# A fused attention, experts and MLP kernel: attention's score products on four 64x64 array tiles, its two heads in two PSUM banks, and a reordered word list

## The chip, the cores and the metric

The kernel runs on one core of a Trainium2 chip. Its time is the device time of one execution in microseconds (us); lower is better. The core has a matrix engine (PE), a vector engine (DVE), a scalar engine (ACT), a third elementwise engine (POOL), and queues of DMA transfers, most of them issued by SP. PE writes its results into PSUM, which has eight banks (0 to 7) of 128 partitions by 512 float32; the other engines read them from there.

## What is computed

Three stages run one after the other in one program, all float32.

```python
# 1. attention: 2 batches, 8 heads, 768 positions, head size 64
k_sum = k.reshape(B, H, 24, 32, D).max(axis=3)          # block maxima of the keys
v_sum = v.reshape(B, H, 24, 32, D).mean(axis=3)         # block means of the values
scores = scale * concat(q @ k.T where |i-j| < 16, q @ k_sum.T) (+ log 32 on the blocks)
x = softmax(scores) @ concat(v, v_sum)                  # 1536 tokens x 512
# 2. four experts, all used: x 512 -> 1024 -> 512, p = domain_probs / their sum
x = sum over e of p[:, e] * (max(x @ w1[e], 0) @ w2[e])
# 3. MLP 512 -> 2048 -> 512
h = x @ w_in;  out = (h * sigmoid(1.702 * h)) @ w_out
```

## The kernel before

**Attention in groups.** Four windows of 64 queries of one pair of heads are a *group*; there are 24 (g = 0 to 23, half of them of the first batch). The two heads of a pair lie on the partition halves 0 to 63 and 64 to 127 of queries and keys. A window of 64 queries needs 96 keys around it and 24 block maxima, so a window's scores have 120 columns. One group goes through these steps, each of them a *word* of the program:

- `sc g` (line 253, PE): eight score products, 4 windows by 2 heads, each 64x64 by 64x120. For groups 0 to 3 two words do this in parts, `dl` with the 96 window columns and `dm` with the 24 block columns (line 270).
- `msk g` (DVE, line 282): reads the scores from PSUM, scales them and adds the mask; then the row maximum (line 287).
- `exp g` (ACT, line 294), `ad g` and `rec g` (the inverse of the sum), `mul g` (DVE or POOL as the letter behind it says, line 314).
- `T g` (PE, line 322): four transposes; `aT g` (ACT, line 328) copies them out.
- `V g` (PE, line 338): eight value products of 64 columns; `xh g` (ACT, line 352) copies them out; `low g` (DVE, line 359) makes the low part for the first batch.
- The block means of the values come by `mp` (POOL), `mq` (DVE), `mt` (PE, line 230), `mk` (ACT), and `vb g` (POOL, line 238) spreads them into the operand of `V g`.

**The experts between them.** While attention of the second batch is still under way, the first expert runs on the first batch: `f i.k` (and `e`, line 455) are first products of hidden unit i, three matmuls each; `ga i` (DVE, line 406), `hh i` (ACT, line 472) and `hl i` (POOL or DVE, line 412) make the gated hidden values and split them into a high and a low part; `s i.d` (line 494) are second products: high by high weights, then low by high weights, then high by low weights. So an `s` needs `hl` from its second matmul on. K, Q, U, N, M, Y, WA and WC are loads on the SP queue; `q0` to `q6` are the first products of the next expert. `x1` words are products whose result nobody reads.

**What sets the order.** A string `ORDER` of 761 words is run from front to back, and each word emits its instructions. Each engine carries out its own instructions in the order in which they were emitted; across engines they wait by semaphores. The framework puts the waits in: who writes a tile in PSUM waits for those who still read the tile's earlier contents.

**Banks.** Scores of all groups but 1 and 2 are in bank 5, head 0 on its upper and head 1 on its lower partition half, so the products use the two array tiles on the diagonal: rows 0 to 63 with columns 0 to 63, rows 64 to 127 with columns 64 to 127. Transposes are in bank 6, value products and the second batch's means in bank 7, the first batch's means and the hidden units from the fifth on (`hidden_bank`) in bank 4. The main part after attention has its two product banks X and Y in 6 and 7.

Of the kernel before, what the change touches and what calls it, by code (L numbers as in the profile page):

```python
# [8 lines left out]
F32 = mybir.dt.float32  # L9
# [4 lines left out]
ALU = mybir.AluOpType  # L14
# [31 lines left out]
def attention_moe_mlp(ctx, tc, kq, vw, vT, dpT, wts, w64, out):  # L46
# [13 lines left out]

    def bank(n, name):
        return psum.tile([P, 512], F32, tag=f"bank{n}", name=name)
# [21 lines left out]
    NM = GW + 2  # L84
# [13 lines left out]
    nc.gpsimd.memset(mask[:, 0, 0 : RAD - 1], NEG)  # L98
    nc.gpsimd.memset(mask[:, NM - 1, WIN + RAD - 1 : KW], NEG)

# [126 lines left out]
    xo = {}  # L227

# [30 lines left out]

    def direct_products(g, c0, c1):  # L260
        b, hp, w0 = g
        k, q = kts[b, hp], qs[g]
        if c0 == 0:
            scs[g] = bank({1: 3, 2: 2}.get(groups.index(g), 5), f"sc{b}{hp}{w0}")
        ps = scs[g]
        for j in range(GW):
            w = (w0 + j) * WIN
            for h in range(2):
                r = slice(h * D, (h + 1) * D)
                nc.tensor.matmul(  # L270
                    ps[r, j * KA + c0 : j * KA + c1],
                    q[r, j * WIN : (j + 1) * WIN],
                    kss[b, hp][r] if c0 else k[r, w : w + KW],
                    start=True, stop=True,
                )

    def masked(g):
# [4 lines left out]
        nc.vector.scalar_tensor_tensor(  # L282
            out=s, in0=ps[:, 0 : GW * KA].rearrange("p (j c) -> p j c", c=KA),
            scalar=1.0 / math.sqrt(D), in1=mask[:, m0 : m0 + GW, :], op0=ALU.mult, op1=ALU.add,
        )
# [45 lines left out]
    def value_products(g):  # L331
        b, hp, w0 = g
        a = st.pop(g)
        v = vs.pop(g)
        ps = st[g] = xo["ps"] = bank(7, f"xo{b}{hp}{w0}")
        for j in range(GW):
            for h in range(2):
                nc.tensor.matmul(  # L338
                    ps[h * D : (h + 1) * D, j * WIN : (j + 1) * WIN],
                    v[0:KA, j, h * D : (h + 1) * D],  # L340
                    a[0:KA, j * P + h * WIN : j * P + (h + 1) * WIN],
                    start=True, stop=True,
                )
# [97 lines left out]
    def hidden_bank(i):  # L441
        return i if i < EARLY else 4
# [318 lines left out]
    def pair(j, extras):  # L761
# [49 lines left out]
        x, y = bank(6, f"X{j}"), bank(7, f"Y{j}")  # L811
# [23 lines left out]
        x = bank(6, f"X{j}b")  # L835
# [22 lines left out]
    def outputs(j, tiles):  # L858
# [62 lines left out]
        def of_half(h):  # L921
# [5 lines left out]
            if h == 0:  # L927
                o = bank(7, "rest")[:, 0 : DM // 2]
# [51 lines left out]
    wlA5:v V5 vb6 ad7:s T6 mk3 gm xh5 vb7 low5 f4.1 aT6 vb8 ps rec7 e2.2 mul7:v win8 e2.3 wb8 win9  # L980
    e2.1 wb9 Q9 pb V6 T7 xh6 sc8 low6 aT7 whC1:s V7 msk8 whC0:s wlC1:g e2.0 xh7 f4.2 low7 exp8
# [17 lines left out]
    T18 sc20 xh16 V17 aT18 hl9:g hl10:g msk20 exp19 Q22 f11.0 ad19:g s8.1 s8.2 f11.1 exp20 win21
    rec19 s8.3 mul19:v U21 f11.2 vb18 win22 f11.3 s9.0 ga11 s9.1 ad20:s s9.2 f12.0 wb21 hh11 hl11:v  # L1000
    ph1 rec20 ph3 xh17 wb22 s9.3 T19 mul20:g sc21 pl3:v aT19 T20 V18 msk21 ph2 xh18 sc22 V19 aT20
    pl1:v Q23 exp21 pc Sa2 win23 wb23 U22 f12.1 vb20 s10.0 U23 msk22 f12.2 f12.3 wBh1 xh19 exp22
    ga12 ad21:g rec21 mul21:v ph0 hh12 sc23 V20 T21 xh20 msk23 f13.0 f13.1 vb21 f13.2 aT21 f13.3
    wBl1:v ad22:g s10.1 rec22 mul22:v exp23 s10.2 ga13 Sa0 ad23:s V21 hh13 pl2:g T22 vb22 rec23
    f14.0 s10.3 mul23:g xh21 f14.1 f14.2 aT22 f14.3 T23 V22 s11.0 aT23 vb23 xh22 hl13:v hl12:v ga14
    V23 pl0:g s11.1 hh14 s11.2 s11.3 xh23 hl14:v f15.0 wo2:v s12.0 s12.1 wo0:v s12.2 wo1:v s12.3
    wo3:v f15.1 f15.2 ra2 s13.0 s13.1 d0 kp d1 f15.3 q0 s13.2 th0 s13.3 s14.0 d2 th1 ga15 q1 tl0:v
    s14.1 mv0 s14.2 hh15 th2 s14.3 tl1:v hl15:g tt0 Ph0 q2 tl2:v d3 mv1 s15.0 s15.1 eu0 eu1 q3 th4
    Sa1 tg0 mv2 Sa3 tl4:v q4 s15.2 tt1 q5 Ph2 wBh0 tg2 eu2 Ph3 Pl2 tr2 tg1 tr0 wBl0:v q6 tw2:v tt2
    Pl0 tr1 Ph1 tw1:g s15.3 tg3 tr3 rb1 Pl3:v eu3 Pl1:v tw3:g tw0:g  # L1010
    """

    xh[0] = slot("xh0", [P, KC, S], F32R, "xh0")
# [287 lines left out]
```

## Time and profile before

| | |
|---|---|
| time, median of 3 runs | 825.35 us (825.27 to 825.8) |
| span of the profiled execution (first to last instruction) | 824.2 us |
| what lies around the span, against the median | 1.15 us |
| PE busy | 817.7 us (99%) |
| DVE / ACT / POOL busy | 577.5 / 412.4 / 409.0 us |
| granted TensorE clock | 1.000 in all slices |

The profiled execution has no separately measured time of its own; 824.2 us is its span, and 1.15 us is the difference to the median of the runs. Attention lies in the first 120 us or so; `q0` starts at 129 us.

### The profile page before, as it was taken

The numbers are of one execution on the slowest core, as the hardware profiler recorded it, in microseconds if no ns is written. First come the engines' busy times: TensorE is split into PE (matmuls) and PEld (weight loads), VectorE is DVE, ScalarE is ACT, GpSimd is POOL, SyncE is SP. The second block draws the span as 40 slices with busy tenths as digits, with TensorE's granted clock in tenths as the row PEclk, the third lists the DMA queues.
The fourth block names the chain that finished last, engine by engine and source line by source line (L and its number), as shares of the span: only waits on it lengthen the run. The fifth ranks groups of instructions, "written<-read, shape, count | busy, mean of one in ns | idle before, by whom it ended". The sixth has DMA issues, their size and how long they took to land.

```text
span 824.2 us, 13712 instructions
## 1 busy us (share of the span) xinstructions
PE 817.7 (99%) x5156; PEld 746.8 (91%) x5156; DVE 577.5 (70%) x859; ACT 412.4 (50%) x958; POOL 409.0 (50%) x374
## 2 busy tenths in 40 slices
PE   9999999999999999999999999999999999999998
PEld 8888899999999999999999999999989988989987
DVE  6787579999988865766676769987688763333332
ACT  5746685545444443443444444446655645434342
POOL 7665642655756522454354366554675743233230
PEclk9999999999999999999999999999999999999999
DMA  8764423967764555587786772223555464733512
GB/s 274 210 201 131 136 72 141 328 227 230 274 243 176 221 223 217 200 315 252 244 323 252 264 252 78 77 78 141 208 170 184 152 239 177 282 121 120 212 40 77
DMA packets 48370, 159.93 MB, mean 194 GB/s; under 512 B 5424, under 2 KB 8752, under 8 KB 43184
## 3 DMA queue, kind: packets, MB, share of 16 engines
q1 hardware_dynamic: 48304, 159.06, 55.3%
q8 instruction: 40, 0.66, 0.3%
q14 instruction: 26, 0.21, 0.1%
HBM read 110.78 MB, written 48.26 MB: 193 GB/s over the span
## 4 chain that ended last, share of the span: by engine, by line
PE 96%; DMA 2%; SPq 1%; DVE 0%; issue 0%; ACT 0%; DVEq 0%
PE o L875 28%; PE Y L748 22%; PE o L906 16%; PE X L748 5%; PE o L494 4%; PE h L455 4%; PE sc L253 2%; PE xo L338 1%; PE at L322 1%; DMA q<-kq 1%; DMA raw_a<-wts 1%; DMA k<-kq 1%; PE pair0y L748 1%; PE X36b L748 0%; PE X42b L748 0%; PE X34b L748 0%
## 5 line engine op out<-in xcount | busy, mean ns | idle before, releaser
L875 PE MATMUL o<-hid,wB 128*128 128x512 f32 x1344 | 260.3, 336 | 0.0
L875 PEld LDWEIGHTS o<-hid,wB 128*128 128x128 f32 x1344 | 214.9, 188 | 20.6
L658 POOL TENSOR_TENSOR wB<-rawB,wB 128x512 fp32r<-128x512 f32 x86 | 118.7, 1390 | 183.0 <-ACT wB L654 168.1
L803 ACT CAST hid<-g 128x384 fp32r<-128x384 f32 x172 | 87.8, 514 | 113.3 <-DVE g L793 79.0
L906 PE MATMUL o<-wB,hid 128*128 128x512 f32 x570 | 135.3, 391 | 0.0
L412 DVE TENSOR_TENSOR hid<-g,hid 128x384 fp32r<-128x384 f32 (+2 forms) x141 | 121.4, 875 | 6.5 <-ACT hid L803 3.0
L906 PEld LDWEIGHTS o<-wB,hid 128*128 128x128 f32 x570 | 106.7, 188 | 21.1
L638 POOL TENSOR_TENSOR wA<-S,wA 128x512 fp32r<-128x512 f32 x44 | 65.4, 1486 | 37.9 <-ACT wA L634 28.4
L638 POOL TENSOR_TENSOR wA<-rawA,wA 128x256 fp32r<-128x256 f32 (+1 forms) x48 | 56.1, 1170 | 51.3 <-ACT wA L634 40.4
L412 POOL TENSOR_TENSOR hid<-g,hid 128x384 fp32r<-128x384 f32 (+2 forms) x51 | 57.0, 1119 | 48.1 <-ACT hid L803 24.1
L793 DVE SCALAR_TENSOR_TENSOR g<-g,pb 128x384 f32<-128x384 f32 x81 | 77.2, 953 | 1.0
L816 ACT COPY prq<-Y 128x384 f32<-128x384 f32 x43 | 20.7, 480 | 104.8 <-PE Y L748 92.5
L748 PE MATMUL Y<-xt,wA 128*128 128x384 f32 x324 | 65.0, 335 | 0.0
L748 PE MATMUL Y<-xh,wA 128*128 128x384 f32 x216 | 63.6, 335 | 0.0
L808 DVE TENSOR_TENSOR g<-X,prq 128x384 f32<-128x384 f32 x43 | 23.8, 554 | 50.5 <-PE X L748 35.8
L831 ACT COPY prq<-Y 128x384 f32<-128x384 f32 x43 | 20.6, 479 | 74.0 <-PE Y L748 74.0
L748 PEld LDWEIGHTS Y<-xt,wA 128*128 128x128 f32 x324 | 53.9, 188 | 2.5 <-ACT prq L826 0.3
L711 POOL TENSOR_TENSOR arena<-arena 128x512 int32<-128x512 int32 x32 | 37.2, 1161 | 36.1 <-ACT arena L701 8.8
L654 ACT CAST wB<-rawB 128x512 fp32r<-128x512 f32 x88 | 52.5, 618 | 2.2 <-DMA rawB<-wts 2.2
L618 DVE TENSOR_TENSOR S<-rawA 128x256 f32<-128x256 f32 x48 | 45.1, 939 | 0.0
L801 DVE TENSOR_TENSOR g<-g,sg 128x384 f32<-128x384 f32 x48 | 35.4, 738 | 11.9 <-ACT sg L800 10.7
L748 PEld LDWEIGHTS Y<-xh,wA 128*128 128x128 f32 x216 | 39.7, 188 | 2.2
(482 smaller groups left out, 1571.2 us busy)
## 6 DMA issues: line engine op xcount, KB each, us to landing
kept<-wA SPq DMA_DIRECT2D x20, 1792.0 KB, 6.8
wA<-kept SPq DMA_DIRECT2D x20, 1792.0 KB, 9.1
arena<-w SPq DMA_DIRECT2D x32, 512.0 KB, 6.0
rawB<-wts SPq DMA_DIRECT2D x28, 512.0 KB, 3.9
rawA<-wts SPq DMA_DIRECT2D x16, 512.0 KB, 7.7
w<-arena SPq DMA_DIRECT2D x32, 256.0 KB, 3.7
rawB<-w SPq DMA_DIRECT2D x16, 512.0 KB, 4.0
rawA<-w SPq DMA_DIRECT2D x8, 512.0 KB, 7.7
```

The lines of the kernel that those rows point to most:

```text
L412: engine.tensor_tensor(out=hl, in0=g, in1=hh.bitcast(F32), op=ALU.subtract)
L618: nc.vector.tensor_tensor(out=t[:, o], in0=a, in1=b, op=op)
L638: engine.tensor_tensor(out=lo, in0=x, in1=hi.bitcast(F32), op=ALU.subtract)
L654: nc.scalar.copy(wB[j][:, 0, f], rawB[j][:, f])
L658: engine.tensor_tensor(out=lo, in0=rawB[j][:, f], in1=hi.bitcast(F32), op=ALU.subtract)
L711: nc.gpsimd.tensor_tensor(out=o, in0=hi, in1=lo, op=ALU.add)
L748: nc.tensor.matmul(ps[:, 0:HS], ws[w], xs[x][:, k], start=(fresh and k == 0 and m == 0), stop=(k == 1 and m == 2), skip_group_check=True,)
L793: nc.vector.scalar_tensor_tensor(out=g, in0=g, scalar=0.0, in1=pbs[ph, s][:, tok], op0=ALU.max, op1=ALU.mult)
L801: nc.vector.tensor_tensor(out=g, in0=c, in1=sg, op=ALU.mult)
L803: heads.append(lambda: nc.scalar.copy(hh, g))
L875: nc.tensor.matmul(o, wB[j][:, w, f, c], tiles[f][:, x, t], start=fr, stop=last, skip_group_check=True,)
L906: nc.tensor.matmul(o, tiles[f][:, x, c], wB[j][:, w, f], start=(new and f == 1 and m == 0), stop=(stops and f == 0 and m == 2),)
```

## The change

Score products: a word's eight matmuls go to all four 64x64 tiles of the array in turn: for each of two pairs of windows, first the even window with head 0 and head 1, then the odd window with head 0 and head 1. The two heads write to two banks, the two windows of a pair to the two partition halves. The banks are shared anew: one tile over banks 4 and 5, `shared_banks`, holds the scores (columns 0 to 239 of either bank, head 0 in 4 and head 1 in 5), the means (bank 4, columns 256 to 383) and the value products (bank 5, columns 256 to 511). Value products of groups 0 to 4 and the first mean are in bank 7, and so are hidden units from the fifth on; X is in bank 7 and Y in bank 6. One mask instruction reads both banks, with one mask for both heads.

```diff
+    XB, YB = 7, 6
...
     def hidden_bank(i):
-        return i if i < EARLY else 4
+        return i if i < EARLY else XB
...
+    shared_banks = att_psum.tile([P, 2, 512], F32, name="att")
+    mean_at, values_at = shared_banks[:, 0, 2 * P : 3 * P], shared_banks[:, 1, 2 * P :]
+    early_bank = bank(XB, "early")
+
+    def scores_of(g):
+        n = {1: (3, 0), 2: (2, 1)}.get(groups.index(g))
+        if n is None:
+            return [shared_banks[:, h] for h in range(2)]
+        return [bank(k, f"sc{h}{g[1]}") for h, k in enumerate(n)]
+
+    def tiles_of_array():
+        return [(j, r, h) for j in range(GP) for r in range(2) for h in range(2)]
 
     def score_products(g):
         b, hp, w0 = g
         k, q = kws.pop(g), qs.pop(g)
-        ps = scs[g] = bank(5, f"sc{b}{hp}{w0}")
-        for j in range(GW):
-            for h in range(2):
-                r = slice(h * D, (h + 1) * D)
-                nc.tensor.matmul(
-                    ps[r, j * KA : (j + 1) * KA],
-                    q[r, j * WIN : (j + 1) * WIN],
-                    k[r, j, :],
-                    start=True, stop=True,
-                )
+        ps = scs[g] = scores_of(g)
+        for j, r, h in tiles_of_array():
+            d, w = slice(h * D, (h + 1) * D), 2 * j + r
+            nc.tensor.matmul(
+                ps[h][r * WIN : (r + 1) * WIN, j * KA : (j + 1) * KA],
+                q[d, w * WIN : (w + 1) * WIN],
+                k[d, w, :],
+                start=True, stop=True,
+            )
...
     def masked(g):
-        nc.vector.scalar_tensor_tensor(
-            out=s, in0=ps[:, 0 : GW * KA].rearrange("p (j c) -> p j c", c=KA),
-            scalar=1.0 / math.sqrt(D), in1=mask[:, m0 : m0 + GW, :], op0=ALU.mult, op1=ALU.add,
-        )
+        if groups.index(g) in (1, 2):
+            parts = [(halves[:, h], ps[h][:, 0:n], m) for h in range(2)]
+        else:
+            parts = [(halves, shared_banks[:, :, 0:n], m.unsqueeze(1).to_broadcast([P, 2, n]))]
+        for o, i, mm in parts:
+            nc.vector.scalar_tensor_tensor(
+                out=o, in0=i, scalar=1.0 / math.sqrt(D), in1=mm, op0=ALU.mult, op1=ALU.add,
+            )
...
     def value_products(g):
-        ps = st[g] = xo["ps"] = bank(7, f"xo{b}{hp}{w0}")
+        ps = st[g] = values_at if groups.index(g) > EARLY else early_bank[:, 2 * P :]
...
     def block_sums(n):
-        mean_ps[n] = bank(7 if b else 4, f"mean{n}")
+        mean_ps[n] = mean_at if n else early_bank
...
-    aT13 rec14 vb12 f8.2 ra0 s5.3 mul14:g f8.3 sc15 vb13 mp7 V12 msk15 T14 hl6:g xh12 V13 aT14 mq7
-    Q19 sc16 xh13 ga8 exp15 win17 wb17 mt7 win18 s6.0 wb18 f9.0 mk7 s6.1 hh8 ad15:g Q20 rec15 msk16
-    mul15:g U16 f9.1 s6.2 U17 vb14 T15 vb15 V14 aT15 sc17 xh14 exp16 V15 msk17 U18 f9.2 s6.3 ad16:s
+    aT13 rec14 vb12 f8.2 ra0 s5.3 mul14:g V12 xh12 f8.3 sc15 vb13 mp7 msk15 T14 hl6:g s6.0 V13 aT14
+    mq7 Q19 xh13 s6.1 sc16 ga8 exp15 win17 wb17 mt7 win18 wb18 f9.0 mk7 hh8 ad15:g Q20 rec15 msk16
+    mul15:g U16 f9.1 vb14 V14 s6.2 U17 xh14 T15 vb15 aT15 sc17 exp16 msk17 U18 f9.2 s6.3 V15 xh15
```

About 25 words of `ORDER` change their place; 761 words stay 761. The instructions themselves show it best. In the rows below, `att` is a tile in the shared banks, `sc`, `xo`, `at`, `mean` are scores, values, transposes and means, `h` and `o` first and second products of the first expert. A number behind a name counts buffers and has no other meaning.

PE before, from `sc15` to `V14` (the product `V12` is the second row, `V13` the fourth):

```order
L253 MATMUL sc_1235<-kw_1205,q_1081 64x120 x8
L338 MATMUL xo_1246<-aT_1142,vw_978 64x64 x8
L322 MATMUL at_1259<-ident,s_1167 120x128 x4
L338 MATMUL xo_1267<-aT_1219,vw_1066 64x64 x8
L253 MATMUL sc_1281<-kw_1212,q_1092 64x120 x8
L230 MATMUL mean_1301<-ident,vsum_108 120x128
L494 MATMUL o_766<-hid_1030,w0ex 128x512 x3
...
L322 MATMUL at_1340<-ident,s_1255 120x128 x4
L338 MATMUL xo_1346<-aT_1276,vw_1207 64x64 x8
```

The row behind the mean is `s6.0`; left out are `s6.1`, `s6.2` and two first products of unit 9 between them. PE of the change, the same stretch, `sc15` to `T15`:

```order
L269 MATMUL att<-kw_1183,q_1064 64x120 x8
L344 MATMUL at_1237<-ident,s_1147 120x128 x4
L517 MATMUL o_756<-hid_1025,w0ex 128x512 x3
L361 MATMUL att<-aT_1197,vw_1050 64x64 x8
L517 MATMUL o_766<-hid_1025,w0ex 128x512 x3
L269 MATMUL att<-kw_1190,q_1075 64x120 x8
L232 MATMUL att<-ident,vsum_108 120x128
...
L361 MATMUL att<-aT_1254,vw_1185 64x64 x8
L517 MATMUL o_783<-hid_1025,w0ex 128x512 x3
L344 MATMUL at_1322<-ident,s_1233 120x128 x4
```

Left out are two first products of unit 9 (six matmuls). `V12` now stands ahead of this stretch, `s6.0` has moved up from behind `sc16` and the mean to between `T14` and `V13`, and `V14` from behind `T15` to ahead of `s6.2`.

PE before, around the transposes of group 21 (`T21`, last row); the three `h` rows are the last of unit 12's first products:

```order
L455 MATMUL h_1622<-xl_117,w0A_103 128x256
L455 MATMUL h_1622<-xh_116,w0A_103 128x256
L253 MATMUL sc_1748<-kw_1708,q_1697 64x120 x8
L338 MATMUL xo_1757<-aT_1694,vw_1529 64x64 x8
L322 MATMUL at_1766<-ident,s_1670 120x128 x4
```

PE of the change, around the same word:

```order
L361 MATMUL att<-aT_1651,vw_1497 64x64 x8
L478 MATMUL h_1596<-xh_121,w0A_103 128x256
L478 MATMUL h_1596<-xl_122,w0A_103 128x256
L478 MATMUL h_1596<-xh_121,w0A_103 128x256
L269 MATMUL att<-kw_1680,q_1654 64x120 x8
L344 MATMUL at_1730<-ident,s_1626 120x128 x4
```

`V20` has moved from between `sc23` and `T21` to ahead of unit 12's last first product, so that between that product and `T21` only `sc23` is left.

## Rows read from the trace of the kernel before

**Rows 1.** The page: span, busy time by engine, and the last chain by engine
```profile
span 824.2 us, 13712 instructions
...
PE 817.7 (99%) x5156; PEld 746.8 (91%) x5156; DVE 577.5 (70%) x859; ACT 412.4 (50%) x958; POOL 409.0 (50%) x374
...
PE 96%; DMA 2%; SPq 1%; DVE 0%; issue 0%; ACT 0%; DVEq 0%
```

**Rows 2.** Waits of PE, whole span: total us, times, longest us
```profile
PE warm L1166 <- DVE raw_b L147: 1.0, 1, 1.0
PE sc L253 <- DMA q<-kq: 0.9, 1, 0.9
PE X L748 <- DVE g L1094: 0.5, 1, 0.5
PE mean L230 <- ACT v_home L1029: 0.3, 1, 0.3
```

**Rows 3.** Timeline of PE, 35.9 to 40 us: start, duration, instruction
```profile
35.98 0.39 PE L455 MATMUL h<-xl,w0A 128*128 128x512 f32 x1
36.21 0.39 PE L455 MATMUL h<-xh,w0A 128*128 128x512 f32 x1
36.53 0.69 PE L338 MATMUL xo<-aT,v_home 120*64 120x64 f32 x16
37.14 0.65 PE L322 MATMUL at<-ident,s 128*120 128x128 f32 x4
37.73 1.04 PE L253 MATMUL sc<-kw,q 64*64 64x120 f32 x16
38.69 0.69 PE L338 MATMUL xo<-aT,vw 120*64 120x64 f32 x16
39.31 0.50 PE L455 MATMUL h<-xh,w0A 128*128 128x512 f32 x1
39.64 0.40 PE L455 MATMUL h<-xl,w0A 128*128 128x512 f32 x1
```

**Rows 4.** Timeline of PE, 9.5 to 12.6 us: the products of window columns
```profile
9.87 0.88 PE L270 MATMUL sc<-k,q 64*64 64x96 f32 x16
10.68 0.71 PE L1166 MATMUL warm<-ident 128*128 128x128 f32 x4
```

**Rows 5.** Timeline of DVE, 39 to 49 us: gates of the first hidden units
```profile
46.05 2.00 DVE L406 SCALAR_TENSOR_TENSOR g<-h,pb 128x512 f32<-128x512 f32 x3
```

**Rows 6.** Timeline of all engines, 77.5 to 90 us, from gate 7 to hl6
```profile
77.68 0.69 DVE L406 SCALAR_TENSOR_TENSOR g<-h,pb 128x512 f32<-128x512 f32 x1
...
79.47 1.30 POOL L412 TENSOR_TENSOR hid<-g,hid 128x512 fp32r<-128x512 f32 x1 [5.96 <-ACT hid L472]
...
79.57 0.28 PE L455 MATMUL h<-xh,w0A 128*128 128x256 f32 x1
...
84.25 0.66 DVE L282 SCALAR_TENSOR_TENSOR s<-sc,mask 128x480 f32<-128x480 f32 x1 [2.52 <-PE sc L253]
...
84.98 1.28 POOL L412 TENSOR_TENSOR hid<-g,hid 128x512 fp32r<-128x512 f32 x1
```

**Rows 7.** The same view, from V13 to the spread means of group 14
```profile
85.33 0.69 PE L338 MATMUL xo<-aT,vw 120*64 120x64 f32 x16
...
86.06 0.37 ACT L352 COPY x<-xo 128x256 f32<-128x256 f32 x1
86.33 0.40 ACT L294 ACTIVATE s<-s,nm 128x120 f32<-128x120 f32 x1
...
89.58 0.61 POOL L238 COPY vw<-vm 24x512 f32<-24x512 f32 x1
```

**Rows 8.** Timeline of all engines, 114.5 to 116.9 us, around T21
```profile
114.86 1.04 PE L253 MATMUL sc<-kw,q 64*64 64x120 f32 x16
...
115.52 0.66 DVE L314 TENSOR_TENSOR s<-s,sm 128x480 f32<-128x480 f32 x1
...
116.45 0.65 PE L322 MATMUL at<-ident,s 128*120 128x128 f32 x4
```

More of the change, by code (lines that the diff above doesn't have):

```diff
@@ L59, in slot @@
         return slots.tile(shape, dt, tag=tag, bufs=bufs, name=name)
+    XB, YB = 7, 6
     def bank(n, name):
-        return psum.tile([P, 512], F32, tag=f"bank{n}", name=name)
+        pool = late[1] if n in (4, 5) else psum
+        return pool.tile([P, 512], F32, tag=f"bank{n}", name=name)
     PIECES = [(0, 2 * GQ), (2 * GQ, S - 2 * GQ)]
@@ L97, in attention_moe_mlp @@
         )
[L98 to L99 removed]
+    nc.gpsimd.memset(mask[0:WIN, 0, 0 : RAD - 1], NEG)
+    nc.gpsimd.memset(mask[WIN:P, NM - 1, WIN + RAD - 1 : KW], NEG)
     kts, qs, vs, vts = {}, {}, {}, {}
@@ L263, in direct_products @@
         if c0 == 0:
-            scs[g] = bank({1: 3, 2: 2}.get(groups.index(g), 5), f"sc{b}{hp}{w0}")
+            scs[g] = scores_of(g)
         ps = scs[g]
[L266 to L274, printed above, removed]
-                )
+        for j, r, h in tiles_of_array():
+            d, w = slice(h * D, (h + 1) * D), 2 * j + r
+            at = (w0 + w) * WIN
+            nc.tensor.matmul(
+                ps[h][r * WIN : (r + 1) * WIN, j * KA + c0 : j * KA + c1],
+                q[d, w * WIN : (w + 1) * WIN],
+                kss[b, hp][d] if c0 else k[d, at : at + KW],
+                start=True, stop=True,
+            )
     def masked(g):
@@ L809, in total_of @@
             return g
-        x, y = bank(6, f"X{j}"), bank(7, f"Y{j}")
+        x, y = bank(XB, f"X{j}"), bank(YB, f"Y{j}")
         cx, cy = x[:, 0:HS], y[:, 0:HS]
@@ L834, in pair @@
         fill(4)
-        x = bank(6, f"X{j}b")
+        x = bank(XB, f"X{j}b")
         cx = x[:, 0:HS]
@@ L927, in of_half @@
             if h == 0:
-                o = bank(7, "rest")[:, 0 : DM // 2]
+                o = bank(YB, "rest")[:, 0 : DM // 2]
             for f in (1, 0):
@@ L999, in attention_moe_mlp @@
[L999 to L1004, printed above, removed]
@@ new lines, in attention_moe_mlp @@
+    hl8:g f10.0 msk18 s7.1 f10.1 win20 s7.2 exp18 rec17 wb20 mul17:g f10.2 s7.3 ra1 vb16 Q21 f10.3
+    V16 ev2 xh16 s8.0 ad18:g ev3 rb0 ga10 T17 rec18 mul18:v sc19 aT17 hh9 ev1 vb19 vb17 msk19 hh10
+    U20 T18 V17 xh17 aT18 hl9:g hl10:g s8.1 s8.2 sc20 exp19 msk20 Q22 f11.0 ad19:g f11.1 exp20 win21
+    rec19 s8.3 mul19:v U21 f11.2 vb18 win22 f11.3 s9.0 ga11 s9.1 ad20:s s9.2 V18 f12.0 wb21 hh11
+    xh18 hl11:v ph1 rec20 ph3 wb22 s9.3 T19 mul20:g sc21 msk21 pl3:v aT19 T20 f12.1 V19 ph2 xh19
+    aT20 pl1:v Q23 exp21 pc s10.0 sc22 msk22 Sa2 win23 wb23 U22 vb20 U23 f12.2 V20 f12.3 wBh1 xh20
@@ new lines, in attention_moe_mlp @@
+    exp22 ga12 ad21:g rec21 mul21:v ph0 hh12 sc23 msk23 T21 f13.0 f13.1 vb21 f13.2 aT21 f13.3 wBl1:v
+    ad22:g s10.1 rec22 mul22:v exp23 s10.2 ga13 Sa0 ad23:s V21 hh13 pl2:g T22 vb22 rec23 f14.0 s10.3
+    mul23:g xh21 f14.1 f14.2 aT22 f14.3 T23 V22 s11.0 aT23 vb23 xh22 hl13:v hl12:v ga14 V23 pl0:g
+    s11.1 hh14 s11.2 s11.3 xh23 hl14:v f15.0 wo2:v s12.0 s12.1 wo0:v s12.2 wo1:v s12.3 wo3:v f15.1
+    f15.2 ra2 s13.0 s13.1 d0 kp d1 f15.3 q0 s13.2 th0 s13.3 s14.0 d2 th1 ga15 q1 tl0:v s14.1 mv0
@@ L1054, in whole @@
             late.append(late_stack.enter_context(tc.tile_pool(name="late", bufs=1)))
+            late.append(
+                late_stack.enter_context(
+                    tc.tile_pool(name="late_psum", bufs=1, space=bass.MemoryType.PSUM)
+                )
+            )
             xt[0] = late[0].tile([P, 2, 3, 2, HS], F32R, tag="xt0", name="xt0")
@@ L1082, in pair0_product @@
         if PRODUCTS[n][2]:
-            banks0[c] = bank(6 if c == "x" else 7, f"pair0{c}{n}")[:, 0:HS]
+            banks0[c] = bank(XB if c == "x" else YB, f"pair0{c}{n}")[:, 0:HS]
         product(banks0[c], 0, *PRODUCTS[n])
```

62 lines of the change are left out of this document (32 added, 30 removed).

## The prediction

> **What bounds the kernel now.** I read the page first. PE is busy for 817.7 of 824.2 us, and the chain that ended last is PE for 96% of the span [rows 1]. The list of PE's waits comes next: four waits, the longest 1.0 us, 2.7 us in all [rows 2]. So the kernel runs at PE's own pace. Two things follow. Every us that PE's instructions get shorter is a us of the result, unless something else is late. And nothing else is late only because the order of the words keeps PE in work until each operand is there; taking work away from PE, or moving a word forward, can open a wait where there was none. Both have to be counted. The sum is made against the profiled execution, span 824.2 us, plus the 1.15 us by which the median of 825.35 us lies above it.
>
> **The score products.** On PE's timeline a group of eight score products begins at 37.73 and the next instruction at 38.69: 0.96 us; another, at 114.86, is shown with the same length [rows 3, 8]. With 96 columns instead of 120 a group takes 10.68 − 9.87 = 0.81 us [rows 4]. The 24 columns cost 0.15 to 0.16 us, 6.5 ns each; the 120 columns then make some 0.79 us, and 0.17 us doesn't depend on columns. Eight matmuls on two tiles are four in a row on each; on four tiles they are two in a row. If the four tiles run beside each other, the columns' part halves, and a group takes 0.40 + 0.17 = 0.57 us: 0.40 less. The bounds are 0.40 us (the constant goes too) and 0.96 us (no gain). I take 0.57, because one row shows that tiles may share their rows: the value products also run on two tiles, which differ in columns and share rows 0 to 119, and eight of them with 64 columns take 37.14 − 36.53 = 0.61 us [rows 3], where the line above gives 64 × 6.5 + 0.17 = 0.59. They overlap as well as the diagonal tiles do.
>
> The Trainium skill speaks against it: "TensorE: Matmul & The Clock Gate", Part 3, says that a weight load overlaps with running matmuls only if its row group differs. Two of the four tiles always share rows, so by this rule a group stays at 0.96 us; the value products, which all share rows, would take about 1.0 us by it, and the row says 0.61. The row decides for me, and the rule is rival 2.
>
> **How many of them count.** 20 words `sc`, and `dl` and `dm` of four groups. The early ones buy nothing: `sc4` waits for a DMA of queries [rows 2], which no edit moves, so what the first products save is spent in that wait; and at 46.05 to 48.05 us DVE is working off three gates in a row that PE's next second products wait for [rows 5]. These gates hang on POOL and ACT work that the new order doesn't shorten. I put the lead that is kept at that point at 0.2 us. Behind it, from the first products of unit 5 to `q0`, 14 `sc` words lie: 14 × 0.40 = 5.6 us.
>
> **Shape switches.** PE pays where products of the small tiles and full-size products meet. A full-size matmul of 512 columns takes 36.21 − 35.98 = 0.23 us with another behind it and 36.53 − 36.21 = 0.32 with value products behind it: entering costs 0.09. Coming back, the first full-size one takes 39.64 − 39.31 = 0.33: leaving costs 0.10 [rows 3]. From transposes (themselves full-size) to full-size products the change is cheaper: transposes followed by scores take 0.59 [rows 3]; I take 0.09 less for each. In the new order small-tile words stand more often alone between full-size ones. Counted over PE's instructions from unit 5 to `q0`, entries rise from 6 to 20, exits from 10 to 20, and transposes with a full-size product behind them from 3 to 6: 14 × 0.09 + 10 × 0.10 − 3 × 0.09 = 2.0 us. PE's work there shrinks by 5.6 − 2.0 = 3.6 us. The two bounds of this term are 5.6 (switches free) and 0 (no gain from four tiles would make it −2.0, rival 2).
>
> **New waits.** The page shows almost no wait, so I looked at what each moved word waits for, and by how much it has moved toward that.
>
> *`s6.0`.* Its second matmul needs the low part `hl6`. POOL reaches it in an unbroken row that begins with the low part at 79.47 and ends at 84.98 + 1.28 = 86.26, and that row begins behind gate 7 (77.68 to 78.37) [rows 6]. In the old order `s6.0` follows `sc16` and the mean, and no wait for POOL is listed [rows 2]. In the new order it follows `T14`. From the first product of unit 8 (79.57 before, [rows 6]) PE has ahead of that second matmul four first products (12 matmuls of half the columns, 0.12 us each), three second products (9 × 0.23), `V12` 0.61, `sc15` 0.57, `T14` 0.45, `s6.0`'s first matmul 0.23 and 0.4 of switches: 5.8 us. The gate is 1.2 us ahead of that first product now, and 0.4 to 1 us in the new order. So `hl6` is there 7.6 to 7.9 us behind the gate, and PE 6.2 to 6.8 us behind it: a wait of 0.8 to 1.7 us; I take 1.3.
>
> *`V14`.* It needs `vb14`, the spread means, which POOL does behind `mul15`. The chain begins with PE's own `V13` at 85.33: ACT copies its result at 86.06 and only then begins `exp15` at 86.33; then come the sum, the inverse, `mul15`, and `vb14` from 89.58 to 90.19 [rows 7]. That is 4.86 us from the start of `V13`. This order on ACT and POOL stays. In the old order `T15` and `s6.2` stand ahead of `V14`, and nothing waits. In the new order PE has `V13` 0.61, `s6.1` 3 × 0.23 and two switches, 0.88, `sc16` 0.57, the mean and two first products (6 × 0.12 and a switch) 0.9, 3.0 us in all. The wait is 1.9 us; its bounds are 0 (if POOL takes `vb14` early) and 1.9.
>
> *`T21`.* It needs `mul21` on DVE, which ends at 115.52 + 0.66 = 116.18, behind a gate that needs the last first product of unit 12, whose successor starts at 114.86. In the old order `sc23` and `V20` fill the time to 116.45 [rows 8]. In the new order `V20` has gone ahead, and `sc23` alone fills 0.57 of 1.33 us: a wait of 0.8 us.
>
> *Bank-wide waits.* The scores, the means and the values are now one tile, so `V g` waits until DVE has read the newest scores (0.12 us behind them and 0.66 long, [rows 6]), and `sc g` until the newest `xh` is out (0.73 us behind the start of `V`, and 0.37 long, [rows 7]). Eight moved words (`mt5`, `T16`, `V16`, `V10`, `V12`, `V20`, `T18`, `V17`) stand in the new order directly behind such a link or one work item behind it. A link is 0.78 or 1.1 us, and what stands between is 0.5 to 1 us. I take 0.3 for each, 2.4 us in all, with bounds of 0 and 6.
>
> The waits sum to 1.3 + 1.9 + 0.8 + 2.4 = 6.4 us.
>
> **What costs nothing.** One mask instruction still reads 480 columns; DVE, 70% busy [rows 1], waits 2.5 us for the scores at 84.25 [rows 6]. Two more mask instructions for groups 1 and 2 lie in the stretch ahead of `sc4`'s DMA. The swap of X and Y moves no work. From `q0` on the chain is PE, so a shift at 129 us goes to the end undiminished.
>
> **Sum.** 824.2 − 0.2 − 3.6 + 6.4 = 826.8, plus 1.15: **828.0 us**, 2.6 us (0.3%) slower. Its own range: 826.2 to 830.5. A measurement of this kernel can tell some 0.2%, 1.65 us.
>
> **Rivals.**
>
> 1. *The waits are covered (faster).* Place: `s6.0`, `V14` and the bank links. If the POOL and ACT chains ahead of these words move forward with PE's shorter score products, or if PE arrives later at them than my counting has it, as after a wait just ahead, the new waits stay under 2 us and the 3.8 us are kept: 825.35 − 3.8 + 0 to 2 = 821.6 to 823.6, with free switches 819.6. It decides at a sum of waits of 3.8 us. For it speaks that a wait at one word is a lead for the next; against it that `V14`'s chain begins with PE itself, so that no delay ahead helps.
> 2. *Four tiles don't run beside each other.* Score groups stay at 0.96, 5.6 us come back, and in the waits that have a score group ahead of them (`s6.0`, `V14`, `T21` and three small ones) 6 × 0.4 = 2.4 us go: 828.0 + 5.6 − 2.4 = 831.2. The rows on value products speak against it. By the Trainium skill's rule in the section named above this is what happens.
> 3. *They cancel.* The waits come to 2.5 to 5.5 us: 824.0 to 827.0, no change that can be told.
>
> **Chances.** My forecast 0.55, of which 0.08 lies below 827.0; rival 1 0.25; rival 2 0.10; rival 3 0.10. Faster 0.25; the same 0.08 + 0.10 = 0.18; slower 0.47 + 0.10 = 0.57. The range for all of them is 821.0 to 831.3: it leaves out the end of rival 1 with free switches (some 0.06) and the upper half of rival 2 with a tail of the forecast (some 0.09).
>
> **What would show it.** PE's timeline: score group to next instruction 0.57 against 0.96. PE's list of waits: second products of line 517 behind POOL's low part, 1 to 2 us; value products of line 361 behind POOL's spread means, up to 1.9 us; transposes of line 344 behind DVE; smaller ones of lines 269 and 361 behind DVE masks and ACT copies. The DMA that ends ahead of `sc4` should end within 0.2 us of where it does now. PE's busy time should fall by some 6 us in all, and its waits grow from 2.7 us to about 10. I am wrong if those waits sum to less than 4 us, or if the score groups don't shrink.

## The result and the profile after

The changed kernel takes 832.04 us (median of 4 runs, 831.0 to 832.64) against 825.51 us (median of 4, 825.27 to 825.8): a ratio of 1.0075, 95% interval 1.0061 to 1.0090. It is slower, by 6.5 us where 2.6 were forecast, and lies 0.7 us above the range. Its profiled execution is the fastest of the four, 831.0 us with a span of 829.2; the three others show a mean granted clock of 0.996 to 0.998.

The page of the changed kernel: span, busy time by engine, and the last chain by engine.

```profile
span 829.2 us, 13733 instructions
...
PE 814.7 (98%) x5156; PEld 738.1 (89%) x5156; DVE 576.8 (70%) x861; ACT 412.7 (50%) x958; POOL 408.8 (49%) x374
...
PE 91%; DVE 3%; POOL 2%; ACT 1%; issue 1%; DMA 1%; SPq 0%; POOLq 0%; DVEq 0%; ACTq 0%
```

Against [rows 1], PE has 3.0 us less work and a span 5.0 us longer, and the chain goes through other engines for 9% of the span instead of 4%. The stretch from unit 5 to `q0` holds nearly all of it. One row of the windows view for this stretch, first of the kernel before, then of the changed one (bounds, length, busy time of PE, PEld, DVE, ACT and POOL with instruction counts, granted clock, DMA share, GB/s):

```profile
48.50:129.20 80.70, 80.70 (x828) 68.64 (x827) 58.15 (x113) 49.88 (x187) 41.12 (x57) 1.00 0.44 136
```

```profile
48.60:134.00 85.40, 78.39 (x828) 62.92 (x827) 59.59 (x113) 50.08 (x188) 40.40 (x58) 1.00 0.40 126
```

PE's 828 instructions shrink from 80.70 to 78.39 us, by 2.3; 7.0 us of idle time come in, where there was none. That is 4.7 of the 5.0 us. The waits of PE in the changed kernel, 48 to 140 us (columns as in [rows 2]):

```profile
PE att L361 <- POOL vw L240: 2.5, 3, 1.9
PE o L517 <- POOL hid L435: 1.4, 1, 1.4
PE at L344 <- DVE s L336: 1.1, 2, 0.8
PE att L361 <- DVE s L305: 0.5, 1, 0.5
PE att L232 <- ACT xh L375: 0.5, 1, 0.5
PE att L232 <- ACT vm L1059: 0.4, 1, 0.4
PE at L344 <- ACT aT L350: 0.3, 1, 0.3
```

The score group itself does what was forecast. PE's timeline of the changed kernel:

```profile
35.56 0.64 PE L269 MATMUL att<-kw,q 64*64 64x120 f32 x16
36.13 0.50 PE L478 MATMUL h<-xh,w0A 128*128 128x512 f32 x1
```

From start to next start it is 0.57 us, where [rows 3] have 0.96. And the two places with the largest waits, timeline of all engines of the changed kernel:

```profile
84.84 0.48 PE L517 MATMUL o<-hid,w0ex 128*128 128x512 f32 x1
...
85.38 1.27 POOL L435 TENSOR_TENSOR hid<-g,hid 128x512 fp32r<-128x512 f32 x1
...
86.70 0.74 PE L517 MATMUL o<-hid,w0ex 128*128 128x512 f32 x2 [1.38 <-POOL hid L435]
87.36 0.69 PE L361 MATMUL att<-aT,vw 120*64 120x64 f32 x16
...
88.10 0.37 ACT L375 COPY x<-att 128x256 f32<-128x256 f32 x1 [2.39 <-PE att L361]
88.37 0.40 ACT L316 ACTIVATE s<-s,nm 128x120 f32<-128x120 f32 x1
...
90.64 0.99 POOL L336 TENSOR_TENSOR s<-s,sm 128x480 f32<-128x480 f32 x1 [0.30 <-DVE sm L332]
...
92.36 0.69 PE L361 MATMUL att<-aT,vw 120*64 120x64 f32 x16 [1.88 <-POOL vw L240]
```

At 84.84 PE does the first of `s6.0`'s three matmuls, and stands 1.38 us until POOL, which began `hl6` at 85.38, is through. `V13` starts at 87.36, ACT copies its result at 88.10 and begins `exp15` at 88.37, POOL scales at 90.64 and then spreads the means, and `V14` can start at 92.36: 5.0 us behind `V13`, as the same chain took 4.86 in [rows 7], while PE had only 3.1 us to do.

### The profile page after: what moved, and what is told of

Its sections match the earlier page's. It is cut to its first block, busy times and chain, and to the rows that moved or that the text cites. A ratio compares the mean times of both kernels' runs of the same rounds, so it can differ in the third digit from the quotient of the medians.

```text
span 829.2 us, 13733 instructions
## 1 busy us (share of the span) xinstructions
PE 814.7 (98%) x5156; PEld 738.1 (89%) x5156; DVE 576.8 (70%) x861; ACT 412.7 (50%) x958; POOL 408.8 (49%) x374
## 4 chain that ended last, share of the span: by engine, by line
PE 91%; DVE 3%; POOL 2%; ACT 1%; issue 1%; DMA 1%; SPq 0%; POOLq 0%; DVEq 0%; ACTq 0%
PE o L898 27%; PE Y L771 21%; PE o L929 16%; PE X L771 5%; PE o L517 3%; PE h L478 3%; PE att L361 1%; PE at L344 1%; PE att L269 1%; POOL s L336 1%; PE warm L1194 1%; PE pair0y L771 1%; DMA q_home<-kq 0%; DVE s L336 0%; DVE g L429 0%
## 5 line engine op out<-in xcount | busy, mean ns | idle before, releaser
L831 DVE TENSOR_TENSOR g<-X,prq 128x384 f32<-128x384 f32 x43 | 23.9, 555 | 50.7 <-PE X L771 35.9
```

## The experiments

Theory A in them: the change shortens PE's work as forecast, and each wait that the new order opens is lost by itself. Theory B: the chains behind PE are late as a whole, so a wait that is removed comes back at the next word. Rivals of single runs stand in their expectations. The kernel before, measured beside them, took 825.62 us (with e1 to e4), 825.47 (e5 to e8) and 825.32 (e9 to e11; medians of 12, 15 and 20). At least 42 of the 761 words stand elsewhere in the new order, not about 25, and the `x` words name other banks.

The span of one profiled execution also hangs on stretches that no run edits. The four-tile kernels with the new words have the same words up to `sc10` and from `q0` on; yet `sc10` starts at 52.85 to 54.30 us, and what lies behind `q0` lasts 694.8 to 695.3 us. So I compare them between these two starts: the changed kernel takes 80.5 us there (53.48 to 133.96), e1 79.7, e2 80.1, e4 78.8, e5 75.3, e9 74.8.

**One wait removed.** Two swaps of words that PE doesn't execute:

```diff
-    mt7 win18 wb18 f9.0 mk7 hh8 ad15:g Q20 rec15 msk16 mul15:g U16 f9.1 vb14 V14
+    mt7 win18 wb18 f9.0 mk7 hh8 vb14 ad15:g Q20 msk16 rec15 mul15:g U16 f9.1 V14
```

> The changed kernel, with two swaps in the word list: POOL spreads the block means of group 14 ahead of scaling group 15's weights, and DVE masks group 16 ahead of the inverse of group 15. Nothing is moved on PE. Theory A (each wait of PE in the changed kernel is lost time by itself): the wait of 1.9 us of the value products of group 14 goes, the span falls from 829.2 to about 827.3 us, and the median by as much, to about 830. Theory B (the chains behind PE are late as a whole, and a wait that is taken away comes back at the next word): the 1.9 us appear at the transposes of group 15 or the value products of group 15, and span and median stay.

Measured: 829.98 us (829.16 to 831.41, 6 runs), span 827.4. The spread means are no longer the last thing that `V14` waits for. PE's waits from 88 to 95 us in this kernel:

```profile
PE att L361 <- POOL sm L327: 0.6, 1, 0.6
PE at L344 <- POOL s L336: 0.2, 1, 0.2
```

1.9 us became 0.6 at `V14` and 0.2 at `T15`. The view names a small POOL word that `V14` doesn't read; of what it needs, the mask of group 16 on DVE ends last, at 90.37. The words `V13`, that mask, `V14` and `sc17`, then `sc17` of the changed kernel:

```profile
86.76 0.69 PE L361 MATMUL att<-aT,vw 120*64 120x64 f32 x16
...
89.71 0.66 DVE L305 SCALAR_TENSOR_TENSOR s<-att,mask 128x480 f32<-128x480 f32 x1 [0.37 <-ACT vm L1059]
...
90.47 0.69 PE L361 MATMUL att<-aT,vw 120*64 120x64 f32 x16 [0.60 <-POOL sm L327]
...
92.85 0.64 PE L269 MATMUL att<-kw,q 64*64 64x120 f32 x16
```

```profile
94.30 0.64 PE L269 MATMUL att<-kw,q 64*64 64x120 f32 x16
```

From `V13` to `sc17` it is 6.09 us instead of 94.30 − 87.36 = 6.94: 0.85 us gained of 1.9. The span fell by 1.8 and the median by 2.1 us, but 0.6 of the span lies ahead of `V13`, where nothing was edited, and against the six later executions of the changed kernel (e11) the median is only 1.2 us lower. So half of this wait goes as theory A says; the rest comes back at the next operand, as theory B says.

**The other wait, by another engine.**

```diff
-    ga7 msk14 T13 ... T14 hl6:g s6.0
+    ga7 msk14 hl6:v T13 ... T14 s6.0
```

> The changed kernel, with the low part of hidden unit 6 on DVE right behind the mask of group 14 instead of on POOL. Theory A: the wait of 1.4 us of the second products of unit 6 goes, span about 827.8, median about 830.6. Theory B: PE waits as much further on, at the mask of group 15 or the spread means of group 14; span and median stay.

Measured: 830.59 us (829.59 to 832.12, 6 runs), span 828.2. Median and span came out near theory A, but between `sc10` and `q0` only 0.4 us of the 1.4 are gained: the wait for `hl6` is gone, and PE's value products wait 3.7 us for spread means instead of 2.5. DVE and POOL of this kernel show why:

```profile
77.43 0.68 DVE L435 TENSOR_TENSOR hid<-g,hid 128x512 fp32r<-128x512 f32 x1
...
79.88 1.42 DVE L435 TENSOR_TENSOR hid<-g,hid 128x512 fp32r<-128x512 f32 x1
```

```profile
79.46 1.30 POOL L435 TENSOR_TENSOR hid<-g,hid 128x512 fp32r<-128x512 f32 x1 [6.45 <-ACT hid L495]
82.23 0.66 POOL L216 COPY kw<-ks 128x96 f32<-128x96 f32 x2 [1.48 <-DVE ks L201]
```

The low part of unit 6 takes 1.42 us on DVE, while the same operation for unit 7 runs on POOL beside it; that of unit 5, at 77.43 with POOL idle, took 0.68. DVE's block maxima come 1.3 us later behind the mask, POOL waits for them, and all that POOL does behind is late. Here theory B is right.

**The words alone.** The kernel before with the new `ORDER`, two tiles and the old banks.

> The kernel before (two array tiles, old banks), with the changed kernel's word list alone. Theory A (waits come from the order of the words and from chains off PE; switches of shape cost 3.0 us; four tiles give 5.5): the three big waits shrink by 0.4 us each because a score group takes 0.97 us, those behind shared banks (some 1.0 us) go, 4 to 5 us of waits stay; span about 824.2 + 3.0 + 4.5 = 831.7. Rival theory C (the waits come from the shared banks): hardly any wait, span about 827.

Measured: 834.92 us (833.88 to 835.96, 6 runs; ratio 1.0107, 1.0089 to 1.0124), span 833.0 at a clock of 0.997. PE waits 4.4 us behind the start-up, as theory A has it in sum. Three of these waits:

```profile
PE xo L338 <- POOL vw L238: 1.8, 1, 1.8
...
PE sc L253 <- PE h L455: 0.8, 1, 0.8
...
PE o L494 <- POOL hid L412: 0.4, 1, 0.4
```

The shared banks are not the cause of the largest wait: `V14` waits as long with the old banks. One by one the waits differ from the expectation: `V14` didn't shrink by 0.4, `s6.0` shrank by 1.0, and in place of `T21` the score products ahead of it wait (second row). The span lies 1.3 us above the forecast; a lower clock, 1.7 us by the rows below, accounts for that much.

**Five places mended at once.** e1's and e2's edits, and:

```diff
-    V11 mq6 ad13:s xh11 mt5 low11 T12 mk5 rec13 mul13:v mt6 aT12 sc14
+    V11 mq6 ad13:s xh11 T12 mt5 low11 mk5 rec13 mul13:v aT12 sc14 mt6
...
-    rec17 wb20 mul17:g f10.2 s7.3 ra1 vb16
+    rec17 wb20 vb16 mul17:g f10.2 s7.3 ra1
...
-    f12.2 V20 f12.3 wBh1 xh20 exp22 ga12 ad21:g rec21 mul21:v ph0 hh12 sc23 msk23 T21 f13.0 f13.1
+    f12.2 f12.3 V20 wBh1 xh20 exp22 ga12 ad21:g rec21 mul21:v ph0 hh12 f13.0 f13.1 sc23 msk23 T21
```

> The changed kernel with four tiles and its banks, and five places of the word list mended: e1's two swaps; e2's low part on DVE; transposes of group 12 ahead of the mean 5 and the score products of group 14 ahead of the mean 6; the spread means of group 16 ahead of the scaling of group 17; and around group 21's transposes two full-size first products moved ahead, so that the last first product of unit 12 comes ahead of the value products of group 20. Theory A: waits of 1.9, 1.4, 0.8, 0.5, 0.85 and 0.35 us go, 5.8 in all; span about 823.4, median between 824.5 and 826, so no slower than the kernel before. Theory B: most waits come back elsewhere, span 827 or more. Should the executions then agree within 0.5 us, with a granted clock of 1.000 in all, then the spread of the changed kernel's runs (831.0 to 832.6) hangs on the waits.

Measured: 828.96 us (828.68 to 830.51, 7 runs), span 827.2: 2.0 us gained of 5.8. Theory B for the rest: `V12` waits 1.4 us for spread means (e2's effect), score products of group 14 wait 0.8 for ACT's copy of a mean, and `f13.0` 0.7 for a gate. As in e2, a word put ahead of others makes those on its own engine later. The executions show clocks of 0.999 and 1.000 and still spread over 1.8 us, so the spread doesn't hang on the clock alone.

**Mended by the rows of e4.** Low part 6 stays on POOL, but goes ahead of two POOL words that nobody waits for soon; the rest are single steps of full-size words to the places where PE stood (`s4.2` ahead of `V10` and e4's edit of `vb16` too):

```diff
-    f8.3 sc15 vb13 mp7 msk15 T14 hl6:g s6.0
+    f8.3 sc15 hl6:g vb13 mp7 msk15 T14 s6.0
...
-    mt7 win18 wb18 f9.0 mk7 hh8 ad15:g Q20 rec15 msk16 mul15:g U16 f9.1 vb14 V14 s6.2 U17 xh14 T15
+    mt7 msk16 f9.0 mk7 hh8 vb14 ad15:g Q20 rec15 win18 wb18 mul15:g U16 f9.1 V14 s6.2 f9.2 U17 xh14 T15
...
-    f7.3 mq5 rec12 s4.3 mul12:v V11 ... s7.0 ga9 T16 sa0 ad17:s sa1 sc18
+    f7.3 mq5 rec12 V11 mul12:v s4.3 ... s7.0 ga9 sc18 T16 sa0 ad17:s sa1
...
-    aT19 T20 f12.1 V19 ... f12.2 V20 f12.3 ... sc23 msk23 T21 f13.0 f13.1
+    aT19 f12.1 T20 V19 ... f12.2 s10.1 V20 f12.3 ... sc23 msk23 f13.0 f13.1 T21
```

> The changed kernel with four tiles and its banks, and the word list mended by what e1, e2 and e4 left: the low part of unit 6 stays on POOL but goes ahead of the spread means of group 13 and the fold of the values; the mask of group 16 ahead of window copies, the spread means of group 14 ahead of the scaling of group 15, one more first product of unit 9 ahead of the transposes of group 15; full-size products ahead of the mean 5, the value products of groups 10 and 20 and the transposes of groups 20 and 21; score products of group 18 ahead of the transposes of group 16; spread means of group 16 earlier. Theory A (every wait of PE is lost by itself and goes when the word it waits for is ready): of the 7.0 us of waits 5.5 to 6.5 go, span 822.7 to 823.7, which is 0 to 1 us below the span of the kernel before at its median time. Theory B (the waits come back elsewhere, since the same number of words has to fill the same chains): span 826 or more, as e4.

Measured: 825.38 us (824.45 to 827.19, 11 runs), ratio 0.9999 (0.9990 to 1.0008), span 823.6. The windows row from unit 5 to `q0`:

```profile
48.30:128.50 80.20, 78.08 (x828) 62.88 (x827) 59.19 (x113) 49.58 (x188) 40.52 (x58) 1.00 0.42 130
```

Idle time is 2.1 us instead of 7.0, PE's work 0.3 less than in the changed kernel. Theory A holds where the word put in the gap was ready and disturbed no other queue. With most of the waits gone, the change as a whole is worth nothing measurable.

**Four more steps of this kind.** `sc14` ahead of `mt6`, `s6.2` ahead of `V14`, `T17` ahead of `s8.0`, `s10.3` ahead of `V21`.

> The kernel of e5, with four more places mended, each by a word that stands a step away: score products of group 14 between the transposes of group 12 and the mean 6, second products of unit 6 ahead of the value products of group 14, transposes of group 17 right behind the value products of group 16, and a second product of unit 10 ahead of the value products of group 21. Theory A: of the 2.0 us of waits that e5 keeps behind unit 5 some 1.5 go; span 822.0 to 822.5, median 0.1 to 0.2% below the kernel before. Theory B: they come back elsewhere, span 823.4 or more.

Measured: 825.15 us (823.89 to 827.95, 12 runs), ratio 0.9993 (0.9981 to 1.0004): no difference that can be told from the kernel before. Its profile had a span of 823.4 with a clock of 0.998; between `sc10` and `q0` it gains 0.5 us on e5. The clock fell at the front, long ahead of any moved word, where this kernel is the same as e5:

```profile
8.00:12.00 4.00, 4.00 (x46) 3.17 (x45) 3.39 (x8) 3.05 (x14) 2.88 (x6) 0.57 1.03 312
```

No version was found that beats the kernel before beyond doubt.

**Two tiles in place of four**, with everything else of the change:

```diff
-                ps[h][r * WIN : (r + 1) * WIN, j * KA : (j + 1) * KA],
+                ps[r][h * WIN : (h + 1) * WIN, j * KA : (j + 1) * KA],
...
-                j, r = h * GP + w // 2, w % 2
+                j, r = (w % 2) * GP + w // 2, h
```

> The changed kernel with its banks and words, but each score product on one of the two tiles on the diagonal: the two heads stay on their own partition halves, even and odd windows go to the two banks. (The mask of the first and last window is then laid over wrong halves.) If four tiles are what shortens a score group from 0.97 to 0.57 us: groups take 0.97 again, 5.6 us of PE work come back behind unit 5, and six waits shrink by 0.4 us each; span 829.2 + 5.6 - 2.4 = 832.4, median about 835. If the two banks and not the tiles shorten a group: groups stay at 0.57 and span and median stay at 829 and 832.

Measured: 835.11 us (834.5 to 837.45, 4 runs), ratio 1.0115. The profiled execution, at a clock of 0.997, has a span of 835.7; the one at 1.000 has 833.1. A score group on its timeline:

```profile
64.41 1.04 PE L269 MATMUL att<-kw,q 64*64 64x120 f32 x16
65.38 0.50 PE L478 MATMUL h<-xh,w0ex 128*128 128x512 f32 x1
```

0.97 us again: having two banks doesn't shorten a group by itself, and with two tiles the same kernel is 3 to 4 us slower. One thing is not parted: in e6 the two heads of a window, which follow each other, write to one bank, as in the kernel before; with four tiles they write to two. No run has a bank for each head on two tiles, or four tiles with both heads in one bank.

**The old words with the new tiles and banks.** The `x` words keep their new banks.

> The changed kernel, four tiles and new banks, with the word list of the kernel before. If the new banks make the moves necessary: value products that stand right behind score products now wait 0.8 us for the mask, score products behind value products 0.5 us for the copy; with some fifteen such places the waits sum to 7 to 10 us, span 824.2 - 4.5 + 8 = 827 to 829. If the shared banks cost little, waits under 3 us and a span of 820 to 822: then the moves alone made the kernel slower.

Measured: 828.9 us (828.5 to 830.23, 5 runs), ratio 1.0044, span 826.7. The windows row from unit 5 to `q0`:

```profile
48.50:131.90 83.40, 76.55 (x828) 63.13 (x827) 59.74 (x113) 50.08 (x188) 40.70 (x58) 1.00 0.41 123
```

6.85 us idle. Of the listed waits 5.1 us stand at words in the shared banks and 1.5 at transposes, which are in bank 6 as before. So the new banks do ask for moves, as this run's expectation says; but the moves as made cost more than they save: the changed kernel takes 2.0 us longer in this stretch.

This row also parts the terms. The words are those of the kernel before, so switches of shape are too, and PE's work should be 80.70 − 5.6 = 75.1 us. It is some 1.4 more, though the score groups that no wait follows are shorter by 0.40 each. Compared word by word with the kernel before, 0.93 us of it lie in the 12 words that stand right ahead of a listed wait, 0.07 to 0.15 each. One of them, value products with a wait behind them:

```profile
111.85 0.69 PE L361 MATMUL att<-aT,vw 120*64 120x64 f32 x16
113.76 0.64 PE L269 MATMUL att<-kw,q 64*64 64x120 f32 x16 [1.23 <-ACT x L375]
```

Without a wait the next word begins 0.61 to 0.62 us behind the start of such a group, though the list shows 0.69 [rows 3]. Here the idle time is counted from the end of the 0.69, so this wait costs 1.30 us and not 1.23. The other 0.5 us lie in words without a listed wait and were not followed. And 78.39 − 76.55 = 1.84 us is the rest, put down to the switches that the new words add, if the extra time is the same in both kernels.

**Waits filled with thrown-away work.**

```diff
-        for j, r, h in tiles_of_array():
+        for j, r, h in tiles_of_array() * {16: 4, 23: 2}.get(groups.index(g), 1):
...
-        for j in range(GW):
+        for j in list(range(GW)) * (4 if groups.index(g) == 14 else 1):
```

> The changed kernel with its waits filled by work that is thrown away: transposes of group 14 four times, score products of group 16 four times and of group 23 twice, the same values to the same place. Theory A: this extra work of about 3.3 us lies in the three big waits, the span stays within 0.7 us of 829.2. On the spread of the runs: if the gaps in PE's work bring the lower clock of some executions, all executions show a granted clock of 1.000 and agree within 0.5 us; if the lower clock comes for another reason, half of them still show 0.996 to 0.999 and lie 0.5 to 2 us above the fastest.

Measured: 833.02 us (832.67 to 833.95, 4 runs), span 832.2, 3.0 us longer, at a clock of 0.998; the others 0.998, 0.998 and 1.000. Neither theory was put to the test. The fill at group 14's transposes took the wait for `hl6`; but score products of group 16 that last longer hold their operand longer, POOL's window copy waits for it, the sum and scaling of group 15 stand behind that copy, and the wait at `V14` is as long as before. PE's waits in this kernel:

```profile
PE att L361 <- POOL vw L240: 2.2, 2, 1.9
```

So the gap was not closed, and the question about the clock was not answered.

**Two gaps in the kernel before.**

```diff
-    T14 hl6:g xh12 V13 ... mt7 win18 s6.0 wb18 ... f9.1 s6.2 U17 vb14 T15 vb15 V14 aT15
+    T14 hl6:g s6.0 xh12 V13 ... mt7 win18 wb18 ... f9.1 vb14 V14 s6.2 U17 T15 vb15 aT15
```

> The kernel before, with two moves of the changed word list alone: the first second product of unit 6 between the transposes of group 14 and the value products of group 13, and spread means and value products of group 14 ahead of the third second product of unit 6 and the transposes of group 15. Two tiles and old banks stay. Theory A: a score group of 0.97 us stands in either gap, so PE waits about 1.0 us at unit 6 and 1.5 us at group 14, two or three switches of shape more; span 823.7 + 2.5 + 0.5 = 826.7. On the clock: if gaps of PE in this stretch bring the lower clock a little later, most executions show a granted clock below 1.000, and the median lies 0.5 to 1.5 us above 828.5; if not, all show 1.000 and the median is 828 to 828.5.

Measured: 828.59 us (827.82 to 831.05, 9 runs), ratio 1.0038 (1.0024 to 1.0051), span 826.3. PE waits 1.6 us at `V14` and 0.7 at `s6.0`. Two moves of the word list cost 3 us in the old kernel. Seven of the nine executions show a clock of 1.000, one 0.999 and one 0.997: these two gaps don't bring the lower clock in most executions.

**The changed kernel again.**

> The changed kernel as it is, on the chip of e9 and e10. If the granted clock below 1.000 in three of its four executions belongs to the kernel, most of these executions show it again, 0.5 to 2 us above the fastest (831.0); if it belonged to the chip or the moment, all lie within 0.5 us of 831.0 with a clock of 1.000.

Measured: 831.17 us (830.24 to 833.15, 6 runs), ratio 1.0061 (1.0043 to 1.0079). Three executions at a clock of 1.000 take 830.24 to 830.39; three at 0.996 to 0.998 take 831.95 to 833.15, so the lower clock comes again, in half of them. The profiled one is at 0.996; its windows, 90 to 100 us:

```profile
90.00:92.00 2.00, 1.29 (x22) 0.92 (x11) 1.14 (x4) 1.47 (x7) 1.20 (x3) 1.00 0.33 70
92.00:94.00 2.00, 0.84 (x17) 0.72 (x17) 0.59 (x1) 0.04 (x1) 1.60 (x3) 0.91 0.61 193
94.00:96.00 2.00, 2.00 (x7) 1.54 (x7) 0.00 (x0) 0.33 (x1) 0.00 (x0) 0.50 0.36 98
96.00:98.00 2.00, 2.00 (x23) 1.47 (x22) 0.59 (x1) 1.56 (x7) 0.56 (x2) 0.74 0.00 0
98.00:100.00 2.00, 2.00 (x25) 1.46 (x23) 1.27 (x5) 1.37 (x9) 0.40 (x1) 1.00 0.00 0
```

PE stands at `V14` until 93.16, and from 94 to 96 us TensorE is granted half its clock (0.50: 1.2 of 2.4 GHz). Over the three windows from 92 to 98 this is 2 × (0.09 + 0.50 + 0.26) = 1.7 us of clock. Not all of this profile's 2.2 us of longer span comes from there: the clock fell in the first 20 us too, as in e9, and `sc16` is already 0.8 us later than in the first profile (89.69 against 88.87); from there to `q0` 1.5 us are added. The first profile of the changed kernel keeps its clock behind the same wait:

```profile
94.00:96.00 2.00, 2.00 (x26) 1.39 (x24) 0.89 (x2) 1.54 (x6) 0.89 (x2) 1.00 0.35 98
```

e3 shows the fall behind its wait of 1.85 us, which ends at 94.05:

```profile
92.00:94.00 2.00, 0.20 (x2) 0.00 (x0) 1.38 (x3) 0.29 (x1) 1.64 (x4) 1.00 0.77 237
94.00:96.00 2.00, 1.95 (x19) 1.60 (x20) 0.00 (x0) 0.37 (x1) 0.55 (x1) 0.64 0.22 46
96.00:98.00 2.00, 2.00 (x15) 1.53 (x15) 0.00 (x0) 0.72 (x2) 0.00 (x0) 0.50 0.24 78
```

## Why the prediction fell short

The sign and the places of the large waits were right, and the waits came out at 7.0 us where 6.4 were forecast. What failed is the sum, in three terms. PE's shortened work, "5.6 − 2.0 = 3.6", came to 2.3, because a wait also costs time that the list counts as work. "Plus the 1.15 us" was too small by 0.65. And the clock, which the sum puts at nothing, cost 1.0 more.

- **Score groups: right.** 0.57 us forecast and measured, 0.40 less for each; with two tiles they take 0.97 again (e6), with what e6 leaves open. The rule of the Trainium skill that was rival 2 ("TensorE: Matmul & The Clock Gate", Part 3: weight loads overlap with running matmuls only across row groups) would by the prediction's reading have left a group at 0.96; the measured 0.57 decides against that for this order of 64x64 tiles.
- **Switches of shape: right, as far as parted.** 2.0 us forecast, 1.84 between e8 and the changed kernel.
- **The three large waits: right.** 1.3, 1.9 and 0.8 us forecast; 1.38, 1.88 and 0.81 measured. Rival 1 (they are covered) fell, for the reason given: `V14`'s chain begins with PE itself.
- **The small waits: the size right, in part by luck.** 2.4 us forecast for eight words, all for the shared banks. Five of these wait, and the mean 6 and `T20` beside them, 2.7 us together; but only `mt5` and `V20`, 1.0 us, wait for a reader of the shared banks as forecast. `V10` and `V16` wait for spread means, `T16` for the scaling, `T20` for ACT's copy of transposes, the mean 6 for the copy of the mean before it. In all it is 7.0 us idle against 6.4.
- **What a wait costs beyond its idle time: missing.** The steps "5.6 − 2.0 = 3.6" and "the waits sum to 6.4" took a wait for what the list shows. By e8 it costs 0.07 to 0.15 us more, and some 1.4 us is missing from PE's saving there with the old words. With 1.84 us of switches that gives the saving of 2.3 in place of 3.6; in the changed kernel itself the two are not parted. The prediction's own sign, PE's busy time some 6 us lower, failed likewise: it fell by 3.0.
- **The lead at the front: −0.2 forecast.** It is 0.1 us the other way. In this profile `sc4` starts at 18.23 us instead of 17.80, and no wait for its DMA is listed any more; ahead of it PE waits 0.6 us for another DMA, that of `q_home`, a wait of 0.5 to 2.3 us in the profiles of the runs that list it.
- **The base: 0.6 us.** The step "plus the 1.15 us by which the median lies above it" took the profiled execution for a median one. In all later runs the time is 1.7 to 1.9 us above the span of the same execution (831.0 and 829.2, for instance). So the profiled execution of before took, by estimate, 826.0 us, 0.5 to 0.65 above its median, and a comparison of its span with the changed one hides that much.
- **The clock: 1.0 us, not thought of.** Median over profiled execution is 832.04 − 831.0. The four executions of the changed kernel at a clock of 1.000 (e11 counted) lie at 830.24 to 831.0, inside the stated range, and the six at 0.996 to 0.998 at 831.65 to 833.15.

From the spans: 829.2 − 824.2 = 5.0, 0.5 of base, 1.0 of clock, together 6.5. Of the 5.0, 7.0 are idle time, −2.3 PE's work, 0.1 the front; 0.2 lie behind `q0`, no more than the runs' profiles differ there. Against the forecast: 1.3 from PE's work, 0.6 from idle time, 0.3 from the front, 0.2 from behind `q0`, 0.65 from the base and 1.0 from the clock make 4.05, and 832.04 lies 4.0 above 828.0.

What stays open: what makes the clock fall. In the four profiles where it does so in this part of the program (e3, e6, e7, e11), it falls behind the wait at `V14`, of 1.85 to 1.87 us there. But the first profile of the changed kernel and that of e2 have the same wait (1.88 and 1.87) and keep 1.00, and so does e10 with 1.6. In e9 and e11 it falls at the front. And the kernel before, whose profile lists hardly a wait, has 4 of its 47 executions beside e1 to e11 at 0.995 to 0.997, with 828.2 to 829.8 us, against six of ten at 0.998 or less here. Whether the wait brings the fall is not settled: the fill that was to tell (e7) didn't close the gap.

## What to carry to other kernels

Where PE never waits, its order is itself a resource: each word hides some chain on another engine, so a faster PE instruction is worth its time only if the chains that it covered are covered by something else; here 5.6 us of shorter products were worth nothing measurable even after the order had been mended. To cost a moved word, measure on the trace the chain from the last PE instruction that starts it to the operand it needs, and set against it what PE has in between: done by hand, this gave three waits within 0.1 us. When a wait is taken away, first look which other queue the word now stands in: half of e1's expected gain and two thirds of e4's went that way. Measure such a gain between two instructions around the edit: a whole span took in 0.6 us from a stretch that e1 hadn't touched.

## What the runs showed that was not expected

- The same subtraction takes 0.68 us on DVE alone and 1.42 us while POOL runs the same operation (e2).
- A wait of PE costs 0.07 to 0.15 us more than its listed idle time (e8): the list counts the last instruction ahead of it at its full length.
- Behind the same wait of PE, 1.87 and 1.88 us, TensorE's granted clock fell to 0.50 in one execution of the changed kernel and stayed at 1.00 in another (e11 and the first profile), and the fall took 1.5 us.
- Changes of shape between 64-row tiles and full-size products cost some 0.19 us for going in and out [rows 3]. The Trainium skill says that changing the tiling mode drains the engine ("TensorEngine Tiling (Array Packing)", Key Properties); the rows agree that it costs, and give this size.
